# Attention with a gated feed-forward: six homes for evicted query and key tiles, the bound in other banks and another place, and moved sums

## The chip, the cores and the metric

The kernel runs on one core of one Trainium2 chip. The metric is the device time of one execution in microseconds (us); times are medians of several runs. The engines are named as in the profile: PE is TensorE (PEld its weight loads), DVE is VectorE, ACT is ScalarE, POOL is GpSimd, and SP issues most of the transfers.

## The reference

The kernel computes a layernorm of x (2048 tokens, 512 columns), a 32-head softmax attention on it, and beside that a SwiGLU feed-forward of width 1792; the result is x plus the attention's output times the silu of the feed-forward's.

```python
def _A_ref(x, wqkv, wo):                      # 32 heads of 16
    qkv = (x @ wqkv).reshape(B, S, 3, H, Dh) ...
    scores = einsum("bhqd,bhkd->bhqk", q, k) * Dh ** -0.5
    o = einsum("bhqk,bhkd->bhqd", softmax(scores), v)
    return o.transpose(...).reshape(B, S, D) @ wo
def _B_ref(x, w_gate, w_up, w_down):
    return (silu(x @ w_gate) * (x @ w_up)) @ w_down
x = A_x                                        # 1 x 2048 x 512
xn = _layernorm(x)
return x + _A_ref(xn, wqkv, wo) * silu(_B_ref(xn, w_gate, w_up, w_down))
```

## The kernel before

**Order.** The order of the instructions on each engine is that of the program text: the scheduler is in manual mode, so an instruction stands in its engine's queue where the code calls it, and an engine works its queue in order. What an instruction waits for (data, a free buffer, a free PSUM bank) is worked out from the tiles that it names.

**Precision.** Matmuls run in a reduced fp32 format. Each operand is split into a high part, which ScalarE casts, and a low part, which VectorE makes by subtraction; a product is high by high, high by low and low by high. Such pairs are xh and xl, whi and wlo, twh and twl (the first and second `split_turn` outputs), guh and gul (the split gate and up weights).

**Prologue.** The first part, up to about 98 us, works on four blocks of 512 tokens: layernorm and transposes on PE, VectorE and ScalarE, the projections to values (`value_tile`) for all of the blocks, and those to queries and keys (`feature_tile`) for the first two. The tiles have numbers `at` from 0 to 31; `step(at, late, ...)` registers a small piece of work that is run before (late 0) or after (late 1) the tile `at`, in the order in which the steps are registered. Blocks 2 and 3 have the tiles 24 to 31. The high and low halves of the normed block 3 are xt_179 and xt_180, in the profile just xt. The value tiles are copied by ScalarE to the staging tile `vt` and stored to v_d. The last of them is accumulated in the bank `extra`.

**Six jobs.** Then the queries and keys of blocks 2 and 3, and two slices of gate and up, are computed by `strassen(i)` for six jobs, in the order qk, qk, feed-forward, qk, qk, feed-forward (below: the first to the last job). A job makes seven products in place of eight: `product` is six matmuls of 128x512 into one of four PSUM banks out of a ring of six (`ring_of`; two of the six are `extra` and `acc`). The products are combined from `spots`: m1 and m5 by ScalarE's copies (line 1030 and 1037), w, u3, c12 and c21 by VectorE (1031, 1041, 1017, 1011), c22 by GpSimd (1042). `sums(i)` makes four sums and differences of job i's raw weights in raw_x (lines 940 to 943), `whole_of(i)` and `summed_of(i)` split the raw weights and the sums in two parts (957, 958, 950, 951, 964, 965). `split_turn(k)` does the same for four sums of the token blocks, made in wide_mr and facc. `between` is a piece that a job runs between its third and its fourth product: the stores of a normed block (`store_x`), the first loads of the attention, or the bound.

**Evictions.** Each of the four qk jobs ends four tiles of 128 features by 512 tokens, 16 evictions in all. `feature_out` squares the tile (ScalarE, 971), casts its high part (ScalarE, 972) and subtracts the low part (VectorE, 973, GpSimd for one of four) into a tile `parts`, stores both parts to q_d or k_d through SP's queue (975), and keeps the maximum of the squares in `top` (VectorE, 976). There are four buffers of `parts`. The first eviction of a job runs in the job, the three others are put in the list `behind` and run in the next job, after its second product.

**The bound.** The softmax uses one shift for everything, worked out from the largest squares. `bound` sums `top` over features with eight small matmuls (`squares`, line 819) into the banks bankx and banky, takes two maxima (1142) and adds them (1143); `spread_shift` makes the shift and a flag out of it and sends it to where the attention reads it. The banks bankx and banky are also those of gate and up, whose matmuls (`fill`, line 290) take the high and low weights guh and gul of `split_gu` (219 and 220); two operations of VectorE (314, 315) end a slice.

**Branch and main loop.** The flag is loaded on every engine (`values_load`, 1153), and a branch (1155) jumps over a general path that isn't taken here. Behind it the pieces still in `behind` run (`first_half`, `second_half`), and the main loop of scores, exponentials and products with the values begins, with the rest of the feed-forward as filler between its matmuls. Its order comes from a planner and isn't touched.

## Time and profile before

| | |
|---|---|
| median of 3 runs | 1398.55 us (1397.57 to 1399.06) |
| profiled execution | 1397.1 us |
| its span | 1395.3 us |
| mean granted TensorE clock | 0.996 |
| TensorE busy | 1376.7 us |
| ScalarE busy | 1169.9 us |
| VectorE busy | 777.1 us |
| GpSimd busy | 146.1 us |

The profile is of one execution, and starts of rows are in us from the span's start. A timeline row gives start, duration, engine, line, operation, output and inputs with their shapes, how many instructions it gathers, and in brackets how long the engine had stood idle before it and what released it. "PEq" or "DVEq" as a releaser is the engine's own sequencer. A waits row gives who waited for whom, the total, how often, and the longest. A windows row gives the busy time and the number of instructions of each engine in a stretch, then the granted clock as a share of full speed, the busy share of the DMA engines, and what they moved. Line numbers of rows are those of the kernel before.

### The profile page before, as it was taken

To read this page: it belongs to the slowest core of one execution; us is meant where nothing else is said; L and a number is where in the kernel's file an instruction comes from. 1 tells how busy PE (TensorE), PEld (TensorE's weight loads), DVE (VectorE), ACT (ScalarE), POOL (GpSimd) and SP (SyncE) were. 2 spreads that over 40 slices of the span, in tenths; PEclk is the share of its full clock that TensorE was granted. 3 is DMA by queue.
4 is the path that set the end of the run, shared out by engine and by line. 5 is a ranking of instruction groups with operands and counts; after the bars stand their busy time and mean duration, and the time that the engine had idled before them with its cause. 6 is when DMAs were issued, how large, how long until landed. Compare 5 with 4: busy or idle time off the path is not lost.

```text
span 1395.3 us, 27442 instructions
## 1 busy us (share of the span) xinstructions
PE 1376.7 (99%) x11020; PEld 854.3 (61%) x11020; DVE 777.1 (56%) x1228; ACT 1169.9 (84%) x1942; POOL 146.1 (10%) x182
## 2 busy tenths in 40 slices
PE   9998899999999999999999999999999999999998
PEld 7877665555665556656566556565556665566555
DVE  7797765535544554466535544563556446656556
ACT  6756468899988998899888889998899889998875
POOL 4335310000000000000010000000100000000142
PEclk9999999999999999999999999999999999999999
DMA  9888665633236433524534355246424113225652
GB/s 300 279 274 263 208 166 118 125 71 93 66 69 137 107 71 76 131 75 105 132 96 99 94 118 119 55 100 124 113 52 97 41 39 74 59 74 160 204 182 84
DMA packets 142868, 169.13 MB, mean 121 GB/s; under 512 B 13850, under 2 KB 87602, under 8 KB 141967
## 3 DMA queue, kind: packets, MB, share of 16 engines
q1 hardware_dynamic: 135198, 141.99, 41.1%
q0 software_dynamic: 7056, 24.78, 5.3%
q8 instruction: 89, 1.46, 0.5%
q10 hardware_dynamic: 480, 0.54, 0.1%
q14 instruction: 45, 0.36, 0.1%
HBM read 119.78 MB, written 45.37 MB: 118 GB/s over the span
## 4 chain that ended last, share of the span: by engine, by line
PE 87%; DVE 0%; DVEq 0%; issue 0%
PE acc L525 32%; PE bankx L290 29%; PE score L1250 10%; PE single L1250 9%; PE banky L290 6%; PE spare L1250 0%; PE spare L1305 0%; PE banky L1305 0%; PE score L1305 0%; DVE y L1312 0%; PE single L1305 0%; DVE facc L1008 0%; DVE y L1318 0%; DVEq L1365 0%
## 5 line engine op out<-in xcount | busy, mean ns | idle before, releaser
L525 PE MATMUL acc<-pr,vst 128*17 128x512 f32 x4096 | 459.5, 593 | 0.0
L1260 ACT ACTIVATE pr<-single 128x512 f32<-128x512 f32 x722 | 411.0, 607 | 9.4 <-PE single L1250 3.8
L1253 ACT ACTIVATE pr<-score 128x1024 f32<-128x1024 f32 x354 | 365.8, 1033 | 27.5 <-PE score L1250 11.0
L525 PEld LDWEIGHTS acc<-pr,vst 128*17 128x17 f32 x4096 | 109.6, 97 | 283.3 <-issue 282.1
L290 PE MATMUL bankx<-fx,guh 64*128 64x512 f32 x832 | 275.4, 393 | 1.4 <-PEq L1155 1.4
L290 PE MATMUL banky<-fx,guh 64*128 64x512 f32 x832 | 275.6, 393 | 0.0
L1257 DVE COPY pr<-spare 128x512 f32<-128x512 f32 x158 | 109.2, 691 | 227.7 <-PE spare L1250 211.8
L1250 PE MATMUL score<-qst,kst 50*128 50x512 f32 x866 | 225.4, 414 | 1.0 <-DVE facc L1008 1.0
L1250 PE MATMUL single<-qst,kst 50*128 50x512 f32 x921 | 213.7, 399 | 0.0
L1270 ACT ACTIVATE pr<-pr 128x512 f32<-128x512 f32 x357 | 198.2, 644 | 0.0
L290 PE MATMUL banky<-wd,hh 64*128 64x512 f32 x672 | 198.0, 392 | 0.0
L290 PE MATMUL bankx<-wd,hh 64*128 64x512 f32 x672 | 197.7, 391 | 0.0
L1257 DVE COPY pr<-single 128x512 f32<-128x512 f32 x199 | 136.9, 688 | 100.3 <-PE single L1250 98.5
L1250 PEld LDWEIGHTS score<-qst,kst 50*128 50x128 f32 x866 | 101.9, 184 | 127.9 <-ACT pr L1260 70.5
L1260 ACT ACTIVATE pr<-score 128x512 f32<-128x512 f32 x158 | 94.9, 601 | 100.9 <-PE spare L1250 92.6
L290 PEld LDWEIGHTS bankx<-fx,guh 64*128 64x128 f32 x832 | 155.3, 187 | 20.2 <-issue 2.2
L290 PE MATMUL bankx<-fx,gul 64*128 64x512 f32 x416 | 163.7, 394 | 0.0
L290 PE MATMUL banky<-fx,gul 64*128 64x512 f32 x416 | 163.6, 393 | 0.0
L290 PEld LDWEIGHTS banky<-fx,guh 64*128 64x128 f32 x832 | 155.4, 187 | 2.5
L1250 PEld LDWEIGHTS single<-qst,kst 50*128 50x128 f32 x921 | 116.6, 185 | 24.6 <-ACT pr L1260 9.7
L290 PEld LDWEIGHTS bankx<-wd,hh 64*128 64x128 f32 x672 | 125.1, 186 | 10.4
L290 PEld LDWEIGHTS banky<-wd,hh 64*128 64x128 f32 x672 | 125.2, 186 | 0.3
(293 smaller groups left out, 1769.1 us busy)
## 6 DMA issues: line engine op xcount, KB each, us to landing
fx<-xt_d SPq DMA_DIRECT2D x48, 512.0 KB
gur<-in_B_w_gate_dram SPq DMA_DIRECT2D x52, 256.0 KB
gur<-in_B_w_up_dram SPq DMA_DIRECT2D x52, 256.0 KB
kst<-k_d SPq DMA_DIRECT2D x192, 64.0 KB
qst<-q_d SPq DMA_DIRECT2D x192, 64.0 KB
q_d<-parts SPq DMA_DIRECT2D x16, 512.0 KB
k_d<-parts SPq DMA_DIRECT2D x16, 512.0 KB
xt_d<-xt POOLq DMA_DIRECT2D x6, 1024.0 KB, 6.6
```

What stands on the lines that cost most here:

```text
L290: mm(bank, lhs[h], rhs[h], start=start, stop=stop)
L525: mm(acc[h * 32:h * 32 + DH + 1], v[:, kt % CT, h * (DH + 1):(h + 1) * (DH + 1)], probs[2 * i + h // 2][:, h % 2], start=tiles[0] == at == ...
L1250: mm(banked[h], k[r, j, kc * P:(kc + 1) * P], q[r, j], start=True, stop=True)
L1253: exps.append(act(pr, both_banks, AF.Exp, scale=0.25))
L1257: dve.tensor_copy(pr[:, h], banked[h])
L1260: exps.append(act(pr[:, h], banked[h], AF.Exp, scale=0.25))
L1270: exps.append(act(part, part, AF.Exp, scale=0.25))
```

## The change

Six things are changed.

1. `feature_out` has six homes for its tiles in place of four: the four buffers of `parts`, and two regions of `vt`. Counted from 1, the evictions 4, 5, 10, 11 and 16 go to `vt`.
2. `bound` takes its banks as an argument: two of the ring of six that the last job doesn't use at that point, in place of bankx and banky. It runs after the last job's fourth product in place of before it.
3. In the last job the gate products (both pieces of `fill`), with `spread_shift` between them, come directly after `bound`, ahead of the last three products. Of `other_half` only the sum c12 stays in the job; its tanh, the two multiplications and the store come after the branch. `split_gu(1)` comes after c12.
4. The sums of the first job's weights are made by VectorE; those of the second job stay on GpSimd, and wait until VectorE has made the second half of the fourth token sum (`fourth`).
5. The steps of tiles 26 to 31 are placed anew: the token sums and their splits come one or two tiles later, the fourth one after the last value tile.
6. The stores of the normed blocks 2 and 3 (two transfers each, GpSimd's queue) run in the second and third job rather than the first and second.

```diff
-        def squares(m, sq):
-            mm(banks[m // 4][(m % 4) * 32:(m % 4) * 32 + 32], ind, sq, start=True, stop=True,
+        def squares(m, sq, to):
+            mm(to[m // 4][(m % 4) * 32:(m % 4) * 32 + 32], ind, sq, start=True, stop=True,
                skip_group_check=True)
...
+        def fourth():
+            turns_x["made"] = dve.tensor_add(wide_mr, wide_mr, b21[1]).ins.name
...
         def sums(i):
...
-            pool.tensor_add(s[:, 0], raw[:, 0], raw[:, 1])
-            pool.tensor_sub(s[:, 1], s[:, 0], raw[:, 2])
-            pool.tensor_sub(s[:, 2], raw[:, 2], raw[:, 0])
-            pool.tensor_sub(s[:, 3], raw[:, 3], s[:, 1])
+            engine = pool if i else dve
+            made = engine.tensor_add(s[:, 0], raw[:, 0], raw[:, 1])
+            if i == 1:
+                tc.add_manual_dep(made.ins, turns_x["made"], settled, reason="GpSimd would hold VectorE up")
+            engine.tensor_sub(s[:, 1], s[:, 0], raw[:, 2])
+            engine.tensor_sub(s[:, 2], raw[:, 2], raw[:, 0])
+            engine.tensor_sub(s[:, 3], raw[:, 3], s[:, 1])
...
         def feature_out(m, b, src, pooled):
-            parts = p3.tile([P, 2, TB], F32R, tag="parts", name="parts")
+            evicted.append(m)
+            at = len(evicted) % 6
+            if at < 4:
+                parts = p3.tile([P, 2, TB], F32R, tag="parts", name="parts")
+            else:
+                n = (at - 4) * 2 * TB
+                parts = vt.rearrange("p g t c -> p (g t c)")[:, n:n + 2 * TB].rearrange("p (s t) -> p s t", s=2).bitcast(F32R)
...
             def other_half():
-                dve.tensor_add(c12, bank[2], w)
+                if more:
+                    dve.tensor_add(c12, bank[2], w)
...
             product(bank[3], summed[2], t3, True, False)
+            if not more:
+                bound([ring_of[(4 * i + n) % 6] for n in (4, 5)])
...
             else:
-                product(bank[2], summed[3], b22, False, True)
-                other_half()
                 fill(3 * DC // 2)
                 spread_shift(ring_of[(4 * i + 4) % 6])
+                fill(3 * DC // 2)
+                product(bank[2], summed[3], b22, False, True)
+                dve.tensor_add(c12, bank[2], w)
                 split_gu(1)
-                fill(3 * DC // 2)
                 product(bank[0], whole[2], b21, False, True)
                 product(bank[3], whole[0], t4, False, True)
                 behind.append(first_half)
                 behind.append(second_half)
+                behind.append(other_half)
...
-        step(26, 1, dve.tensor_sub, wide_mr, upper_x, lower_x)
+        step(27, 1, dve.tensor_sub, wide_mr, upper_x, lower_x)
         for j in range(2):
-            step(27, j, dve.tensor_sub, lower_x, lower_x, b11[j])
+            step(28, 0, dve.tensor_sub, lower_x, lower_x, b11[j])
         step(28, 0, dve.tensor_sub, upper_x, upper_x, lower_x)
-        step(28, 0, whole_of, 0)
+        step(28, 1, sums, 0)
+        step(28, 1, whole_of, 0)
         step(28, 1, split_turn, 0, upper_x)
         step(29, 0, split_turn, 1, lower_x)
-        step(29, 0, summed_of, 0)
-        step(29, 1, split_turn, 2, wide_mr)
-        step(30, 0, dve.tensor_sub, wide_mr, b21[0], upper_x)
-        step(30, 0, dve.tensor_add, wide_mr, wide_mr, b21[1])
-        step(30, 1, split_turn, 3, wide_mr)
-        step(27, 0, sums, 0)
+        step(29, 1, summed_of, 0)
+        step(30, 0, split_turn, 2, wide_mr)
+        step(31, 1, dve.tensor_sub, wide_mr, b21[0], upper_x)
+        step(31, 1, fourth)
+        step(31, 1, split_turn, 3, wide_mr)
...
-        def bound():
+        def bound(to):
             for m in range(8):
-                squares(m, top[m])
+                squares(m, top[m], to)
             for j in range(2):
-                dve.reduce_max(peak[:, j:j + 1], banks[j], axis=AX.X)
+                dve.reduce_max(peak[:, j:j + 1], to[j], axis=AX.X)
...
-            strassen(i, {0: partial(store_x, 2), 1: partial(store_x, 3), 3: first_loads, len(jobs) - 1: bound}.get(i))
+            strassen(i, {1: partial(store_x, 2), 2: partial(store_x, 3), 3: first_loads}.get(i))
```

On VectorE, around the value tiles of block 3, before; xt_180 is the block's low half, the line 742 is that of all the steps, and facc and wide_mr hold the token sums:

```order
L742 TENSOR_TENSOR xt_180<-facc,xt_179 128x512 x3
L742 TENSOR_TENSOR wide_mr<-facc 128x1024
L742 TENSOR_TENSOR facc<-facc,xt_177 128x1024
L742 TENSOR_TENSOR xt_180<-facc,xt_179 128x512
L742 TENSOR_TENSOR facc<-facc,xt_178 128x1024
L742 TENSOR_TENSOR facc<-facc 128x1024
```

and now:

```order
L742 TENSOR_TENSOR xt_180<-facc,xt_179 128x512 x4
L742 TENSOR_TENSOR wide_mr<-facc 128x1024
L742 TENSOR_TENSOR facc<-facc,xt_177 128x1024
L742 TENSOR_TENSOR facc<-facc,xt_178 128x1024
L742 TENSOR_TENSOR facc<-facc 128x1024
L944 TENSOR_TENSOR raw_x<-raw 128x256
L947 TENSOR_TENSOR raw_x<-raw_x,raw 128x256
L948 TENSOR_TENSOR raw_x<-raw 128x256
L949 TENSOR_TENSOR raw_x<-raw,raw_x 128x256
```

The fourth subtraction for xt_180 has moved ahead of two of the token sums, and the four sums of the first job's raw weights have come in behind the token sums.

On ScalarE, at the end of the value tiles, before; twh are the high parts of the token sums, extra is the bank of the last value tile, and the copy to spots is the first of the first job:

```order
L895 COPY vt<-ps 128x8x4x16
L934 CAST twh_992<-wide_mr 128x1024
L895 COPY vt<-ps 128x8x4x16
L934 CAST twh_1012<-wide_mr 128x1024
L895 COPY vt<-extra 128x8x4x16
L1030 COPY spots<-ps 128x512
```

and now:

```order
L970 CAST part<-raw_x 128x1024
L937 CAST twh_992<-wide_mr 128x1024
L895 COPY vt<-ps 128x8x4x16
L895 COPY vt<-extra 128x8x4x16
L937 CAST twh_1029<-wide_mr 128x1024
L1042 COPY spots<-ps 128x512
```

The copy out of extra has moved ahead of the cast of the fourth token sum.

On TensorE, in the last job at the end of the bound's small matmuls, before; acc and ps are ring banks:

```order
L819 LDWEIGHTS ind
L819 MATMUL banky<-top_171,ind 32x512
L1002 MATMUL acc<-twh_992,part 128x512
L1002 MATMUL acc<-twl_993,part 128x512
L1002 MATMUL acc<-twh_992,part 128x512 x2
L1002 MATMUL acc<-twl_993,part 128x512
L1002 MATMUL acc<-twh_992,part 128x512
L1002 MATMUL ps<-xt_179,part 128x512
```

and now:

```order
L819 LDWEIGHTS ind
L819 MATMUL ps<-top_171,ind 32x512
L290 MATMUL bankx<-fx,guh 128x512
L290 MATMUL banky<-fx,guh 128x512
L290 MATMUL bankx<-fx,guh 128x512
L290 MATMUL banky<-fx,guh 128x512
L290 MATMUL bankx<-fx,gul 128x512
L290 MATMUL banky<-fx,gul 128x512
```

What follows the last small matmul was the job's fourth product and is now the gate products with guh and gul; the small matmuls write a ring bank.

On VectorE, in the last job from the shift to the branch, before; s_226, flag and shift are the shift's steps, ga the gate's, guh and gul the split weights of the next gate slice, facc and raw_x those of the job:

```order
L1021 SCALAR_TENSOR_TENSOR raw_x<-raw_x,facc 128x512
L1129 TENSOR_REDUCE s_226<-ps 1x1
L1130 TENSOR_SCALAR s_226<-s_226 1x1
L1131 TENSOR_SCALAR flag<-s_226 1x1
L1132 TENSOR_SCALAR shift<-row,s_226 1x512
L219 CAST guh<-gur 128x1024
L220 TENSOR_TENSOR gul<-gur,guh 128x1024
L314 SCALAR_TENSOR_TENSOR ga<-th,bankx 128x512
L315 SCALAR_TENSOR_TENSOR ga<-ga,banky 128x512
L1153 TENSOR_LOAD flag
L1155 COMPARE_AND_BRANCH
```

and now:

```order
L1055 TENSOR_TENSOR spots<-acc,spots 128x512
L1144 TENSOR_REDUCE s_226<-ps 1x1
L1145 TENSOR_SCALAR s_226<-s_226 1x1
L1146 TENSOR_SCALAR flag<-s_226 1x1
L1147 TENSOR_SCALAR shift<-row,s_226 1x512
L314 SCALAR_TENSOR_TENSOR ga<-th,bankx 128x512
L315 SCALAR_TENSOR_TENSOR ga<-ga,banky 128x512
L1082 TENSOR_TENSOR facc<-ps,spots 128x512
L219 CAST guh<-gur 128x1024
L220 TENSOR_TENSOR gul<-gur,guh 128x1024
L1168 TENSOR_LOAD flag
L1170 COMPARE_AND_BRANCH
```

The sum of c12 (line 1082 in the changed kernel) and the split of the next slice have moved behind the two gate operations, directly ahead of the branch; the two multiplications into raw_x have gone from here.

## Rows read from the trace of the kernel before

**Rows 1.** Page, busy time of each engine: us, share of the span, instructions.
```profile
PE 1376.7 (99%) x11020; PEld 854.3 (61%) x11020; DVE 777.1 (56%) x1228; ACT 1169.9 (84%) x1942; POOL 146.1 (10%) x182
```

**Rows 2.** TensorE's waits: what for, us in total, times, longest.
```profile
PE banky L819 <- DVE top L976: 3.1, 2, 2.4
PE extra L1002 <- ACT spots L1030: 2.3, 1, 2.3
PE extra L1002 <- ACT vt L895: 1.9, 1, 1.9
PE ps L814 <- DVE xt L742: 1.7, 3, 0.8
PE ps L1002 <- DVE parts L973: 1.6, 1, 1.6
PE bankx L290 <- PEq L1155: 1.4, 1, 1.4
...
PE score L1250 <- DVE facc L1008: 1.0, 1, 1.0
```

**Rows 3.** Windows: us, busy of PE, PEld, DVE, ACT, POOL; clock, DMA share, GB/s.
```profile
164.00:168.00 4.00, 3.24 (x8) 1.93 (x7) 3.96 (x6) 0.94 (x2) 0.00 (x0) 0.50 1.01 380
168.00:172.00 4.00, 4.00 (x18) 2.93 (x18) 2.15 (x5) 0.38 (x1) 1.28 (x1) 0.69 0.23 90
184.00:188.00 4.00, 4.00 (x24) 3.71 (x21) 3.38 (x5) 2.97 (x5) 3.84 (x4) 0.57 0.67 203
```

**Rows 4.** Timeline of VectorE to the second job: start, us, operation, [idle before <-releaser].
```profile
78.78 1.82 DVE L742 TENSOR_TENSOR xt<-raw_x,xt 128x512 fp32r<-128x512 f32 x2
...
90.46 1.23 DVE L742 TENSOR_TENSOR facc<-facc,xt 128x1024 f32<-128x1024 f32 x1
...
92.75 1.75 DVE L742 TENSOR_TENSOR facc<-facc,xt 128x1024 f32<-128x1024 f32 x1
...
109.47 0.69 DVE L1041 TENSOR_TENSOR spots<-ps,spots 128x512 f32<-128x512 f32 x1 [0.88 <-PE ps L1002]
...
119.06 1.08 DVE L958 TENSOR_TENSOR whole<-raw,whole 128x256 fp32r<-128x256 f32 x3
```

**Rows 5.** Timeline of TensorE, first to last job.
```profile
106.41 0.50 PE L1002 MATMUL extra<-twh,part 128*128 128x512 f32 x1 [1.88 <-ACT vt L895]
...
112.05 0.39 PE L1002 MATMUL ps<-twh,whole 128*128 128x512 f32 x1
...
154.71 1.54 PE L1002 MATMUL extra<-xt,odd 128*128 128x512 f32 x6
...
160.77 0.40 PE L819 MATMUL bankx<-top,ind 128*32 128x512 bf16 x4
...
176.65 0.39 PE L290 MATMUL bankx<-fx,gul 64*128 64x512 f32 x1
```

**Rows 6.** Timeline of GpSimd, the sums of the third job's weights.
```profile
114.00 0.73 POOL L942 TENSOR_TENSOR raw_x<-raw 128x256 f32<-128x256 f32 x1
```

**Rows 7.** Timeline of ScalarE, casts of evictions 13, 14 and 16.
```profile
157.83 0.58 ACT L972 CAST parts<-ps 128x512 fp32r<-128x512 f32 x1 [5.04 <-DMA q_d<-parts]
...
160.24 0.62 ACT L972 CAST parts<-facc 128x512 fp32r<-128x512 f32 x1 [1.29 <-DMA q_d<-parts]
...
163.35 0.62 ACT L972 CAST parts<-facc 128x512 fp32r<-128x512 f32 x1 [0.20 <-DMA q_d<-parts]
```

**Rows 8.** Timeline of VectorE, fifth job to the branch.
```profile
165.54 0.68 DVE L219 CAST guh<-gur 128x1024 fp32r<-128x1024 f32 x1
166.26 1.23 DVE L220 TENSOR_TENSOR gul<-gur,guh 128x1024 fp32r<-128x1024 f32 x1
...
178.50 0.69 DVE L315 SCALAR_TENSOR_TENSOR ga<-ga,banky 128x512 f32<-128x512 f32 x1
182.21 0.69 DVE L1008 SCALAR_TENSOR_TENSOR facc<-facc,extra 128x512 f32<-128x512 f32 x1 [3.03 <-DVEq L1155]
```

**Rows 9.** Page, DMA issues: count, KB each, us from issue to landing.
```profile
xt_d<-xt POOLq DMA_DIRECT2D x6, 1024.0 KB, 6.6
```

More of the change, by code (lines that the diff above doesn't have):

```diff
@@ L976, in feature_out @@
             dve.tensor_max(top[m], top[m], sq)
-        behind = []
-        ring_of = []
+        behind, ring_of, evicted = [], [], []
         def strassen(i, between=None):
```

## The prediction

> **What bounds the kernel now.** I read the page's busy line first: TensorE is busy 1376.7 us of 1395.3, VectorE 777.1 [rows 1]. So only time in which TensorE stands still, or runs at the lower of its clock's two levels, can be won. The main loop, from about 183 us to the end, is a gapless stream in which the change moves nothing, so all of the difference has to come from the first 190 us. Second, TensorE's waits by releaser [rows 2]: in this part there are 13.0 us of them on seven lines that the change touches. In order of time they are: the value tiles of blocks 2 and 3 behind VectorE's layernorm (1.7), the first job's fourth product behind an eviction (1.9), the third job behind ScalarE (2.3), the fifth job's ring bank behind a cast (1.6), the bound's small products behind the last maxima (3.1), and the two around the branch (1.4 and 1.0). Third, the windows [rows 3]: from 164 to 172 us the granted clock averages 0.50 and then 0.69. [...] Another such stretch, 0.57, follows the branch.
>
> The profiled execution took 1397.1 us, 1.8 more than its span, and the median of the three runs is 1398.55. I sum against the profiled one and take the difference off the median, since everything changed lies inside the span.
>
> **First job: moved steps and sums.** The waits at the value tiles go if all works. The longest of the three, 0.8, is for the last subtraction that makes xt_180, which now follows its three fellows directly (two subtractions of 1.2 us less ahead of it on VectorE, as the one at 90.46 [rows 4]). The other two, 0.9 together, are for the pair at 78.78, which took 1.82 us beside GpSimd's first sums [rows 4]; those sums leave GpSimd. And 1.9 us go at extra, since ScalarE's copy out of extra no longer stands behind the cast of twh_1012, which waits for VectorE. That is 3.6. What is late next is VectorE. Its chain in the first job ends with the sum u3 at 109.47 [rows 4], which waited 0.88 us for TensorE; without that it starts at 108.59 and ends at 109.28. The seventh product, which writes the bank that u3 reads, began at 112.05 [rows 5]; so it can come at most 2.8 earlier. Does the chain itself grow? The four sums that VectorE takes over are a quarter-size each: three such operations take 1.08 us, so four take 1.4 [rows 4]. Against that, three subtractions of 1024 columns ran at 1.65 to 1.75 us beside GpSimd's sums, where a free one took 1.23 [rows 4]; those sums now wait behind fourth, so 3 x 0.5 = 1.5 comes back. That is even. But the same GpSimd sums now run later, beside the split of twl_1030, odd and u3, and lengthen one or two of them by the same 0.5. I take 0.4 off: **2.4 us won**, bounds 1.5 (two operations lengthened, and the next job's split weights late by 0.3) and 3.6 (VectorE not in the way).
>
> The row says that such a neighbour stretches an operation by 0.5 us [rows 4]. [...]
>
> **Six homes.** A cast of eviction n waits until the transfer of n-4 has left its buffer; now it waits for n-6. Evictions 7 and 8 then wait for 1 and 2, long landed, and the 2.3 us at extra in the third job [rows 2] goes: **2.3 won**, since ScalarE's queue there holds nothing else that is late. In the fifth job eviction 13's cast waited 5.04 us for eviction 9's transfer [rows 7]; it now looks at 7's, and TensorE's 1.6 us behind it [rows 2, 5] goes: **1.6 won**. The bound from below is nothing, if another transfer is as late. The two homes in the value staging tile are covered by its stores, which are over before.
>
> **Bound in banks of its own, three products later.** The last of eight small products waits for the last maximum. Eviction 16's cast, at 163.35, can't come before eviction 10's transfer lands; that landing is what released the cast at 160.24 [rows 7]. From the start of the last cast to the end of VectorE's cast to guh there were 2.87 us (163.35 to 166.22), to the end of gul 4.14 [rows 7, 8]. So in the new order, and on the old time axis, guh is there at 163.11 and gul at 164.38. TensorE has the four products from 154.71 on done at 160.23, at 1.38 each [rows 5]. Its stretch from there to gul is 4.15; in it lie eight small products, about 1.0 us by four in 0.40 with their loads [rows 5], and two pairs of gate products, 0.46. So 2.7 us of waiting are left against 3.1 [rows 2]: **0.4 won**. If the transfers land in time, all but nothing is waited: 3.1 won. The gate products that now fill the place behind the small products need guh and gul, which stand on VectorE behind the maximum; that is why the wait is not hidden.
>
> **The clock.** At 164 to 168 us TensorE was busy 3.24 us at 0.50, which cost 1.62; at 168 to 172 it was 4.00 at 0.69, which cost 1.24 [rows 3]. Together 2.9 won if no dip stands there. But 2.7 us of wait remain in nearly the same place, and after the branch a wait of that size was followed by 0.57 over 4 us, a cost of 1.7 [rows 3]. I take such a dip as likely: **1.2 won**, bounds 0 and 2.9.
>
> **The tail before the branch.** The products of c12, which came before the gate stretch, stand behind it, and VectorE's sum c12 and the split of gul (with guh) come after the two gate results. Let T be the end of the last gate product, 177.04 before [rows 5]. TensorE then has three products, 4.2, then the branch, 1.35, and filler 0.7: it is at the score at T+6.3. VectorE ends the second gate operation at T+2.14 (178.50+0.69), then c12 0.6, guh 0.7, gul 1.2: T+4.7. Behind the branch it stood still 3.03 us, then first_half's operation of 0.69 [rows 8]. The score waits for that, as it did for 1.0 us [rows 2]: it can start at about T+8.6. That is 2.3 of waiting where there was 1.0: **1.3 lost**. Bounds: 0 lost, and 2.0 if other_half's tanh, now also behind the branch, gets ahead of something. other_half's store and the memsets on GpSimd behind it are needed some 20 us later and cost nothing.
>
> [...] The row says a branch costs VectorE 3.03 us of standing still [rows 8]. [...]
>
> **Small.** Five waits fewer each save the slower first product behind a wait, 0.50 against 0.39 [rows 5]: **0.5 won**. The two stores of x blocks move one job later, to where the evictions' transfers run; I put that at nothing, and its price is rival E.
>
> **Sum.** 2.4 + 2.3 + 1.6 + 0.4 + 1.2 - 1.3 + 0.5 = 7.1 us, so 1397.1 becomes 1390.0 and the median 1398.55 becomes **1391.4**.
>
> **The rivals.** **B**, transfers land early: fewer collisions ahead of eviction 10, no wait at the bound and no dip. Then 2.7 and 1.7 come on top: a gain of 11.5, 1387.0; for it speaks that evictions start earlier, against it that four jobs' casts waited for transfers. **C**, the clock stays low as long as before, and GpSimd's moved sums cost the first job their full bound: 1.2 and 0.9 less, a gain of 5.0, 1393.5; 1394.3 if the stretch behind the branch is longer too. For it speaks that the wait at the bound keeps nearly its size. **D**, the homes were not the limit: the transfers are, each cast waits as long one home later, and the clock falls as before. Without 2.3, 1.6, 0.4 and 1.2 the gain is 1.6: 1396.9, no measurable change. For it speaks the DMA share of 1.01 at 164 to 168 [rows 3], against it that the wait of 5.04 is for a transfer four evictions back. **E**, slower: the x-block stores, 1 MB each and 6.6 us from issue to landing [rows 9], get ahead of eviction 10's transfer. TensorE pays in full for each us that this lands later, since the bound waits for eviction 16 and that for 10. Slower by more than 0.2% from 9.9 us later; two stores in its way are 13.2: 1404.6. Against it: the stores are issued 30 us before. **F**, VectorE's branch is cheap: the tail's wait is gone, 2.3 more, 1389.1.
>
> **How the numbers follow.** A change under 0.2%, about 2.8 us, can't be told from none. Forecast 50%, B 15%, C 22%, D 7%, E 3%, F 3%. Only D lies within 0.2%, only E above: faster 0.90, same 0.07, slower 0.03. The range runs from 1386.8, B's time with a little of the first term's upper bound, to 1394.6, C's upper end with as much; it leaves out D, E and the outer part of B.
>
> **What would show it.** Right: no waits at the value tiles, at extra in the first job and in the third; eviction 13's cast not waiting for a transfer; a wait of 2 to 3 us at the small products or at the first gate products behind guh; a clock below 1 for about 4 us behind it; the score waiting 2 us or more for VectorE. Wrong: a wait of the second job for its split weights behind GpSimd's sums (first term), eviction 16's cast released by something other than a transfer (fourth term, B), a clock of 1 up to the branch (fifth), casts in the second to fourth job waiting for transfers (D, E).

## The result, and the profile after

The changed kernel takes 1400.74 us in the median of 20 runs (1399.16 to 1402.51), the kernel before, in 20 runs beside it, 1397.63. The ratio is 1.0022, with a 95% interval from 1.0015 to 1.0029: slower by 3 us, where 1391.4 was forecast. The profiled execution took 1399.16 us, its span 1397.4. Line numbers below are those of each kernel's own code; in the changed one 1013 stands for 1002, 988 for 976, 1055 for 1041, 1265 for 1250, 1268 for the exponential (1253).

The page's busy line, which answers to [rows 1]:

```profile
PE 1377.4 (99%) x11020; PEld 852.8 (61%) x11020; DVE 779.1 (56%) x1232; ACT 1169.7 (84%) x1942; POOL 141.7 (10%) x178
```

TensorE is as busy as before within 1 us, so the difference is again mostly in its waits. Those of the changed kernel, in the form of [rows 2]:

```profile
PE ps L819 <- DVE top L988: 4.3, 2, 2.2
PE score L1265 <- ACT pr L1268: 3.4, 1, 3.4
PE score L1265 <- DVE facc L1019: 1.5, 1, 1.5
PE ps L1013 <- DVE spots L1055: 1.5, 3, 0.8
PE bankx L290 <- PEq L1170: 1.3, 1, 1.3
...
PE bankx L290 <- DVE guh L219: 0.6, 1, 0.6
PE ps L1013 <- ACT spots L1042: 0.5, 1, 0.5
```

All that was to go has gone: the value tiles' 1.7 us (0.3 is left, behind ScalarE), the 1.9 and the 2.3 at extra, the 1.6 at a ring bank. In their place the jobs have five short waits behind spots, for u3 and for ScalarE's copies, 2.4 us together (1.5, 0.5 and 0.4). The small products wait 4.3 us rather than 3.1, and one line is new and large: the second scores behind the branch wait 3.4 us for ScalarE. What ScalarE waited for there is in its timeline (start, duration, operation, idle time before and releaser):

```profile
159.08 0.62 ACT L984 CAST parts<-facc 128x512 fp32r<-128x512 f32 x1 [4.25 <-DMA q_d<-parts]
...
161.54 0.62 ACT L984 CAST vt<-facc 128x512 fp32r<-128x512 f32 x1 [1.31 <-DMA q_d<-vt]
...
185.86 1.02 ACT L1268 ACTIVATE pr<-score 128x1024 f32<-128x1024 f32 x1 [8.41 <-DMA h_d<-raw_x]
```

The third row is the main loop's first exponential. ScalarE had been idle for 8.4 us, and what released it is the store of h_d out of raw_x. SP's timeline shows when that store was issued:

```profile
183.73 0.33 SPq L1034 DMA_DIRECT2D h_d<-raw_x  x1
```

It is other_half's store, which the change put behind the branch. It lands about 2 us after its issue, and the exponential starts then. TensorE's seventh product of the first job, against 112.05 in [rows 5]:

```profile
109.61 0.50 PE L1013 MATMUL ps<-twh,whole 128*128 128x512 f32 x1 [0.24 <-DVE spots L1055]
```

TensorE's two stretches at the lower clock, 0.50 where it is 1.00 just ahead of them and behind them, in the form of [rows 3], before:

```profile
163.60:170.40 6.80, 5.90 (x13) 3.90 (x13) 5.51 (x10) 1.34 (x3) 0.74 (x1) 0.50 0.80 296
184.10:187.50 3.40, 3.40 (x20) 3.13 (x18) 3.21 (x4) 2.41 (x4) 3.24 (x4) 0.50 0.60 190
```

and now:

```profile
162.80:169.60 6.80, 5.62 (x23) 3.52 (x24) 4.86 (x9) 0.33 (x1) 1.27 (x1) 0.50 1.08 368
186.70:190.10 3.40, 3.16 (x15) 3.01 (x17) 2.71 (x4) 3.08 (x6) 3.24 (x4) 0.50 1.07 225
```

By starts in the two traces the changed kernel is ahead by 2.4 us at that seventh product, by 4.0 at the last job's third product (155.18 against 159.19), and by 1.9 at the first score (181.18 against 183.10). At 200 us it is behind by 1.6, and so it stays for most of the loop (2.1 at the end). So where the forecast had 6.3 us (2.4 + 2.3 + 1.6), 4.0 were there. Half of these were lost between the third product and the first score, and 3.5 us more went between 181 and 192 us.

### The profile page after: what moved, and what is told of

Its sections match the earlier page's. It is cut to its first block, busy times and chain, and to the rows that moved or that the text cites. A ratio compares the mean times of both kernels' runs of the same rounds, so it can differ in the third digit from the quotient of the medians.

```text
span 1397.4 us, 27445 instructions
## 1 busy us (share of the span) xinstructions
PE 1377.4 (99%) x11020; PEld 852.8 (61%) x11020; DVE 779.1 (56%) x1232; ACT 1169.7 (84%) x1942; POOL 141.7 (10%) x178
## 4 chain that ended last, share of the span: by engine, by line
PE 86%; DVE 0%; DMA 0%; ACT 0%; DVEq 0%; issue 0%; ACTq 0%
PE acc L525 32%; PE bankx L290 28%; PE score L1265 10%; PE single L1265 8%; PE banky L290 6%; PE spare L1265 1%; PE spare L1320 0%; PE banky L1320 0%; DMA h_d<-raw_x 0%; ACT pr L1268 0%; PE score L1320 0%; DVE raw_x L1033 0%; DVE y L1327 0%; PE single L1320 0%; DVE facc L1024 0%; DVE facc L1019 0%
```

## The experiments

Each run has its own runs of the kernel before beside it (medians 1396.8 to 1397.4), so ratios are compared where a few us matter. One per cent is 14 us.

**One address.** The last job's g2 in a tile of the gate's pool, not in raw_x:

```diff
-            g2 = wide_mr[:, 0] if more else raw_x[:, 0]
+            g2 = wide_mr[:, 0] if more else two.tile([P, TB], F32, tag="ga", name="g2")
```

> The changed kernel (1400.7), with one address changed: the last job's product g2, which other_half stores behind the branch, lies in a tile of the pool of gate results rather than in raw_x. Nothing moves on any engine. Theory (the loss sits behind the branch: the main loop's first exponential takes over memory of the prologue's pool, and so waits for the store out of raw_x): ScalarE's wait for the store goes, TensorE's 3.4 us at the second pair of scores too, and 1 to 1.7 us of low clock behind it; 1395.5 to 1397. Rival (the loss is the bound's longer wait and the order of the last job): another wait takes the store's place, 1400 to 1401.

Measured 1399.27 us, ratio 1.0014 (1.0003 to 1.0024), and its eleven runs are spread from 1395.9 to 1402.1. TensorE's waits, and VectorE's timeline behind the branch:

```profile
PE ps L819 <- DVE top L988: 4.5, 2, 2.6
PE single L1265 <- DVE pr L1272: 3.5, 1, 3.5
PE score L1265 <- DVE facc L1019: 2.7, 1, 2.7
```

```profile
184.37 1.23 DVE L220 TENSOR_TENSOR gul<-gur,guh 128x1024 fp32r<-128x1024 f32 x1
189.58 0.43 DVE L234 CAST wd<-wdr 128x512 fp32r<-128x512 f32 x1 [3.98 <-DMA kst<-k_d]
```

The wait for the store is gone, as the theory said, and the first exponential waits for nothing but its scores. But the time is not: VectorE now stands for 4.0 us at the cast of the first down weights (wd), and TensorE for 3.5 us behind a copy of VectorE's that is queued behind this cast. The releaser is named as a load of kst, which shares a semaphore with the load of wdr; the cast waits for wdr. SP issued that load only behind the two stores of the last job, which wait for VectorE. Its place in the queue isn't all of it: it was issued at 183.3 and landed about 6 us later, where the one of the changed kernel, issued at 184.1, took about 3. Behind TensorE's wait the clock is at 0.50 from 192 to 199 us, which it is not in the changed kernel. The rival is not borne out by this, but neither is the theory's size.

**The last job as before**, the rest as changed:

```diff
...
-            if not more:
-                bound([ring_of[(4 * i + n) % 6] for n in (4, 5)])
...
+                product(bank[2], summed[3], b22, False, True)
+                other_half()
                 fill(3 * DC // 2)
                 spread_shift(ring_of[(4 * i + 4) % 6])
-                fill(3 * DC // 2)
-                product(bank[2], summed[3], b22, False, True)
-                dve.tensor_add(c12, bank[2], w)
                 split_gu(1)
+                fill(3 * DC // 2)
...
-                behind.append(other_half)
...
-            strassen(i, {1: partial(store_x, 2), 2: partial(store_x, 3), 3: first_loads}.get(i))
+            strassen(i, {1: partial(store_x, 2), 2: partial(store_x, 3), 3: first_loads, len(jobs) - 1: partial(bound, banks)}.get(i))
```

> The changed kernel with the last job as it was before: the bound in bankx and banky ahead of the fourth product, the gate products behind the third product of bank 2, all of other_half ahead of the branch. Homes, steps, sums and stores stay changed. Theory: the store is ahead of the branch again, so the 3.4 us go; the last maximum comes 1.8 us earlier than in the kernel before, since the last cast does; about 1395.8, as far as e1. Rival (late transfers are what costs, wherever the store stands): 1399 to 1401.

Measured 1394.71 us, ratio 0.9984 (0.9975 to 0.9993): 5.3 us below the changed kernel by the ratios. So the last job's new order, with all that it moved behind the branch, costs more than the whole loss. The wait at the small products is longer than in either kernel:

```profile
PE banky L819 <- DVE top L988: 5.6, 2, 3.7
```

**Four homes:**

```diff
-            at = len(evicted) % 6
+            at = 0
```

> The changed kernel with four homes for evictions, as before. Theory (the homes won what was forecast): the waits of 2.3 us in the third job and 1.6 us in the fifth come back, less up to 0.9 us of VectorE's waits that they hide, and the last cast waits for eviction 12 at about 163.4: 1402.5 to 1404.5. Rival (transfers, not homes, are the limit): 1400 to 1401.5.

Measured 1401.5 us, ratio 1.0029 (1.0018 to 1.0041). The waits of the third and the last job are back at 2.9 and 1.8 us, but those at the small products and gate products shrink to 3.0 from 4.9 and the one for the exponential to 2.1. In the changed kernel the homes win about 1 us in all, which is not clear of none: what they win is waited for again at the bound. The time is the upper edge of the rival's range, and at the bound the transfers are indeed the limit.

**The stores of blocks 2 and 3 where they were:**

```diff
-            strassen(i, {1: partial(store_x, 2), 2: partial(store_x, 3), 3: first_loads}.get(i))
+            strassen(i, {0: partial(store_x, 2), 1: partial(store_x, 3), 3: first_loads}.get(i))
```

> The changed kernel with the stores of the normed blocks 2 and 3 in the first and second job, as before. Theory (they made evictions 9 and 10 land 1.3 us late): the casts of 15 and 16 start 1.3 us earlier, TensorE's wait at the small products is 3.6 rather than 4.9 us: about 1399.4. Rival (the early stores collide with the first evictions' transfers and the weights' loads): no earlier landing, a wait in the second or third job, 1400.7 to 1403.

Measured 1396.43 us, ratio 0.9996 (0.9987 to 1.0005): 3.6 us by the ratios, more than the theory's 1.3. ScalarE's cast of eviction 16, and TensorE's waits:

```profile
157.46 0.62 ACT L984 CAST vt<-facc 128x512 fp32r<-128x512 f32 x1 [1.09 <-DMA q_d<-vt]
```

```profile
PE score L1265 <- DVE facc L1019: 2.7, 1, 2.7
PE score L1265 <- ACT pr L1268: 2.5, 1, 2.5
...
PE ps L819 <- DVE top L988: 0.9, 1, 0.9
PE bankx L290 <- DVE guh L219: 0.8, 1, 0.8
```

The cast starts at 157.46 rather than 161.54, so the transfer of eviction 10 lands 4.1 us earlier, and the waits of 4.9 us at the bound become 1.9 (with 0.2 for gul). Moving 4 MB of stores one job later is what made it late. SP's timeline shows how. The changed kernel:

```profile
139.12 6.19 SPq L185 DMA_DIRECT2D kst<-k_d  x6
...
154.24 0.93 SPq L987 DMA_DIRECT2D q_d<-vt  x2
```

and this run:

```profile
138.32 2.75 SPq L185 DMA_DIRECT2D kst<-k_d  x6
...
150.41 1.42 SPq L987 DMA_DIRECT2D q_d<-vt  x2
```

The first of the two q_d stores is eviction 10's. It takes about as long in both runs (7.3 us from its issue to the cast, and 7.1), but is issued 3.8 us later in the changed kernel. The moved stores are not in its way: the last of them, issued at 128.3, had landed 12.5 us later, 13 us before eviction 10 was issued. What they slow are the stores to k_d that are issued beside them: the last two of the job land 12.7 and 14.0 us after their issue rather than 7.9 and 8.2. SP's first six loads of K (line 185) take 6.2 us rather than 2.8, since they stand 2.0 us for that landing and 1.5 for other transfers; and eviction 10 stands behind these loads on SP's queue. Neither this run nor the kernel before has a wait at line 185 from 126 to 158 us; the changed kernel's largest is:

```profile
SPq L185 <- DMA k_d<-parts: 2.0, 2, 1.7
```

All the other kernels with the late stores (e1, e2, e3 and e13) have it too, at 1.5 to 2.2 us, and none of those with the early ones.

**Both undone**, the edits of e2 and e4; then that kernel with the edit of e3, and with the sums as before:

```diff
-            engine = pool if i else dve
+            engine = pool
...
-            if i == 1:
-                tc.add_manual_dep(made.ins, turns_x["made"], settled, reason="GpSimd would hold VectorE up")
...
-        step(28, 1, sums, 0)
...
+        step(27, 0, sums, 0)
```

> The changed kernel with both parts undone that the first runs point to: the last job as before, and the stores of blocks 2 and 3 in the first and second job. Homes, sums and steps stay changed. Theory (two separate losses, the store behind the branch with what the last job's new order brings, 6 us, and the late landings, 4 us): the small products wait 1.5 to 2 us rather than 5.6, the clock dips less; 1390 to 1392. Rival (one loss, seen twice: what the landing wins is lost again at the bound in its old place): 1394 to 1396.

> e5 with four homes. Theory (with the stores out of the way the homes are worth the two waits of 2.3 and 1.6 us, and the cast of eviction 16 waits for 12): 3 to 5 us slower than e5, 1394 to 1396. Rival (the homes only move the wait to the bound, as in e3): within 1 us of e5.

> e5 with the sums of the first job's weights back on GpSimd, two tiles earlier, and those of the second job not held back. Steps stay in their new order. Theory (the first term's two halves, of which the sums carry the subtractions at 78 and 92 us): the two waits of 0.9 us at block 2's value tiles come back, and VectorE's three long subtractions: 1 to 2 us slower than e5. Rival (VectorE's u3 is late in three later jobs anyway and hides it): within 0.5 us of e5.

Measured 1391.35 (e5, ratio 0.9960, 0.9946 to 0.9974), 1397.05 (e6, 1.0000, 0.9991 to 1.0009) and 1389.86 us (e7, 0.9951, 0.9937 to 0.9965). The losses add up: e5 is the changed kernel less 8.7 us, against 5.3 and 3.6 of the two edits alone. With the transfers out of the way the homes are worth 5.7 us. In e6 the wait of the third job is back, and the one at the small products is longer (2.5 in e5):

```profile
PE extra L1013 <- ACT spots L1041: 3.3, 1, 3.3
PE banky L819 <- DVE top L988: 3.2, 2, 2.3
```

The waits are not all of the 5.7. Behind the first of them TensorE runs at the lower clock, which it does neither in e5 nor in the kernel before in that job:

```profile
129.60:136.40 6.80, 5.43 (x13) 4.27 (x14) 5.01 (x8) 5.15 (x7) 2.67 (x2) 0.50 1.06 352
```

TensorE is busy for 5.4 us there at half the clock, so 2.7 us are lost.

The sums on VectorE win nothing; e7 is 1.5 us faster without them by the medians, which neither of its expectations had. It has 1.4 us of waits at block 2's value tiles again, but the seventh product of the first job starts at 109.35 in e7 and at 109.32 in e5, so what won the first term were the moved steps. And in e5 ScalarE's cast of the second job's sums waited 2.1 us for GpSimd's held sums, in e7 for nothing:

```profile
109.29 1.05 ACT L970 CAST part<-raw_x 128x1024 fp32r<-128x1024 f32 x1 [2.10 <-POOL raw_x L949]
```

```profile
107.35 1.06 ACT L968 CAST part<-raw_x 128x1024 fp32r<-128x1024 f32 x1
```

**The sums not held**, as e5 but without the wait on `fourth`:

```diff
-            if i == 1:
+            if i == 9:
                 tc.add_manual_dep(made.ins, turns_x["made"], settled, reason="GpSimd would hold VectorE up")
```

> e5 without the hold on the second job's sums (they start on GpSimd as soon as their weights are there); the first job's stay on VectorE. Theory (the hold is what cost e5 its 1.5 us against e7: the second job's split of sums and with it ScalarE's copies came late): 1389.5 to 1390.5, as e7. Rival (the four sums on VectorE cost it): 1391 to 1392, as e5.

Measured 1392.4 us, ratio 0.9964: no better than e5. It was not the hold; with the first job's sums on VectorE, the waits come back at other places (0.9 us for a split of sums, 1.3 for a copy of ScalarE's). That VectorE's own 1.5 us are the cost agrees with all three runs; more is not shown.

**All ahead of the branch.** The stores early, g2 in a gate tile as in e1, evictions 15 and 16 behind the last job's own copies and sums, the first load of down weights in the job, and the job in this order:

```diff
-            while behind:
+            while len(behind) > (0 if more else 2):
                 behind.pop(0)()
...
+            while not more and behind:
+                behind.pop(0)()
...
             else:
-                fill(3 * DC // 2)
-                spread_shift(ring_of[(4 * i + 4) % 6])
-                fill(3 * DC // 2)
                 product(bank[2], summed[3], b22, False, True)
                 dve.tensor_add(c12, bank[2], w)
                 split_gu(1)
+                fill(3 * DC // 2)
+                bound([ring_of[(4 * i + n) % 6] for n in (4, 5)])
+                fill(3 * DC // 4)
+                spread_shift(ring_of[(4 * i + 4) % 6])
+                fill(3 * DC // 4)
+                load_wd(0, 0)
                 product(bank[0], whole[2], b21, False, True)
+                first_half()
                 product(bank[3], whole[0], t4, False, True)
-                behind.append(first_half)
-                behind.append(second_half)
-                behind.append(other_half)
+                second_half()
+                other_half()
```

> The changed kernel with the early stores and another order of the last job: the evictions 15 and 16 stand on ScalarE and VectorE behind the job's copies and sums, the third product of bank 2 and one half of the gate products ahead of the bound, the other half, two products and all of first_half, second_half and other_half behind it and ahead of the branch; g2 in a gate tile; the first load of down weights issued ahead of the branch. Theory (all waits from the fourth product to the second score are for casts, for splits behind maxima, and for pieces behind the branch): TensorE waits for nothing from 152 us to the branch, the first score comes at about 171 us rather than 181, no low clock: 1384 to 1388. Rival (the landing of eviction 10 or the branch's own 3 us on VectorE take the place): 1390 or more.

Measured 1394.78 us, ratio 0.9982 (0.9973 to 0.9991). TensorE waits for nothing at the bound, but there is a new wait, and SP's timeline shows it:

```profile
PE score L1267 <- SPq L1173: 6.2, 1, 6.2
PE ps L1146 <- DVE sm L1161: 2.0, 1, 2.0
```

```profile
175.79 0.32 SPq L1034 DMA_DIRECT2D h_d<-g  x1
180.38 0.72 SPq L212 DMA_DIRECT2D gur<-in_B_w_gate_dram  x1
```

SP issues the last store at 175.79, and its next transfer behind the branch comes 4.6 us later. Until then the first score can't start: it waits on what SP announces behind the branch. Of the 4.6 us, 1.3 lie ahead of SP's own branch (177.1), and 2.7 between it and SP's first instruction behind it (179.8). The store's landing is not what is waited for: from 178.3 to 180 us no DMA packet moves at all, and in the kernel before SP stood 2.6 us at the branch (178.8 to 181.3) without a store just ahead of it. The loss is that SP comes to the branch late, 4.2 us after TensorE's last product, since it first issues the stores, and the last of them waits for VectorE's last multiplication (to 175.8). VectorE, with the same work ahead of its branch, is late with it: it starts again at 179.8.

**other_half in the job**, in the changed order with early stores (e4 with its store ahead of the branch):

```diff
-                dve.tensor_add(c12, bank[2], w)
+                other_half()
                 split_gu(1)
...
-                behind.append(other_half)
```

> The changed kernel with the early stores (e4, 1396.4) and all of other_half in the job, ahead of the split and of the branch; the rest of the last job in its new order. Theory (the store behind the branch is the larger part of what the new order costs): ScalarE doesn't wait for the store, TensorE's 2.5 us at the second scores go and the low clock behind them, two operations more on VectorE ahead of the branch cost up to 1.4: 1392.5 to 1394.5. Rival (as in e8 the store's landing then holds SP's branch and the first score): 1395.5 to 1397.

Measured 1396.19 us, ratio 0.9992 (0.9983 to 1.0001), its runs from 1393.5 to 1398.4: no gain over e4, as the rival said, though by another engine:

```profile
PE score L1263 <- DVE facc L1019: 5.1, 1, 5.1
```

```profile
173.05 1.23 DVE L220 TENSOR_TENSOR gul<-gur,guh 128x1024 fp32r<-128x1024 f32 x1
177.99 0.69 DVE L1019 SCALAR_TENSOR_TENSOR facc<-facc,extra 128x512 f32<-128x512 f32 x1 [3.71 <-DVEq L1168]
```

The store's wait is gone, and VectorE, with two operations more, ends its work 2.4 us later than TensorE; then it stands 3.7 us at the branch, and the first score waits 5.1 us for it.

**Stores behind, but out of the way.** e8 with the two stores and the products ahead of them behind the branch again, c21 ahead of it, the split of gul behind the shift, and the load of down weights ahead of the bound; then the same with e7's sums:

```diff
-                split_gu(1)
                 fill(3 * DC // 2)
+                load_wd(0, 0)
                 bound([ring_of[(4 * i + n) % 6] for n in (4, 5)])
                 fill(3 * DC // 4)
                 spread_shift(ring_of[(4 * i + 4) % 6])
+                split_gu(1)
                 fill(3 * DC // 4)
-                load_wd(0, 0)
                 product(bank[0], whole[2], b21, False, True)
                 first_half()
                 product(bank[3], whole[0], t4, False, True)
-                second_half()
-                other_half()
+                dve.tensor_add(c21, bank[3], w)
+                behind.append(second_half)
+                behind.append(other_half)
```

> e8 with what its trace points to: there the first score waited 6.2 us for SP, whose branch stood behind the two stores of the last job and their landing, and TensorE 2.0 us for a maximum behind the split of gul. Here both stores and the products ahead of them stand behind the branch again, but out of memory that the main loop doesn't take over (a gate tile), c21 ahead of the branch, the split behind the shift. Theory (what the branch waits for is what SP has under way): the first score at 171 to 173 us, no wait for SP over 2 us: 1385 to 1388. Rival (it is the branch itself that costs SP and ScalarE 4 us and more): 1391 to 1395.

> e9 with the sums on GpSimd as in e7. Theory (the gain of e7 lies in the second job and adds up): 1 to 2 us faster than e9. Rival (it is lost at the casts' landings): within 0.5 us of e9.

Measured 1389.15 (e9, ratio 0.9942, 0.9929 to 0.9956) and 1386.67 us (e10, 0.9925, 0.9912 to 0.9939). Both are faster than either kernel, the second by 10.6 us than the one before. The sums make 2.5 us here. What is left in e10 at the branch:

```profile
PE bankx L290 <- PEq L1173: 3.1, 1, 3.1
PE score L1267 <- DVEq L1173: 1.0, 1, 1.0
```

The branch itself, 3.1 us on TensorE (3.5 in e9), is now the largest of its waits. e9's time lies between its theory's range and the rival's. The first score comes at 174.3 us rather than at 171 to 173, and SP still stands 3.5 us at the branch (168.2 to 171.7), with no store just ahead of it. In e8 most of SP's 2.7 us went by with no packet moving, so the landing of what SP has under way isn't the main part of this cost. Whether it makes the 0.8 us more of e9 is open.

**The changed kernel less what was found behind the branch**, e1 with the first load of down weights ahead of the last two products; and with early stores too:

```diff
+                load_wd(0, 0)
                 product(bank[0], whole[2], b21, False, True)
...
-    load_wd(0, 0)
```

> e1 (1399.3, its runs 6 us apart) with the first load of down weights issued ahead of the last two products rather than behind the branch and the two stores on SP's queue. Theory (what took the store's place in e1 is VectorE's 4.0 us for those weights, whose load lands early in some runs and late in others): the wait goes, and the runs lie within 2 us of each other; 1394.5 to 1396.5. Rival (the low clock behind the bound and the branch holds the time, whatever waits there): 1398 to 1400.

> e13 with the early stores of blocks 2 and 3: the changed kernel with its order, its sums and its steps, less the three things found behind the branch and on the queues. Theory (the losses are separate): e4's 1396.4 less TensorE's 2.5 us for the store and some low clock, 1391 to 1393.5. Rival (the first score's 2.7 us for VectorE grow into it): 1394 to 1396.

Measured 1395.04 (ratio 0.9987, 0.9978 to 0.9996) and 1391.36 us (0.9961, 0.9947 to 0.9975). VectorE in e13 goes from gul to wd without a wait:

```profile
183.98 1.22 DVE L220 TENSOR_TENSOR gul<-gur,guh 128x1024 fp32r<-128x1024 f32 x1
185.12 0.42 DVE L234 CAST wd<-wdr 128x512 fp32r<-128x512 f32 x1
```

That closes e1: the store and the load of weights behind it make 4.9 us by the ratios. (The runs of e13 still lie 3.4 us apart, not 2.) The early stores make 3.6 more. e14 keeps the changed order, sums and homes, and its waits and windows show the bound nearly covered and the clock at full there; a stretch at 0.50 is left behind the branch, where TensorE had waited 2.8 us:

```profile
PE score L1265 <- DVE facc L1019: 2.8, 1, 2.8
...
PE bankx L290 <- DVE guh L219: 0.8, 1, 0.8
PE ps L819 <- DVE top L988: 0.6, 1, 0.6
PE bankx L290 <- DVE gul L220: 0.5, 1, 0.5
```

```profile
160.00:164.00 4.00, 3.12 (x24) 2.13 (x24) 3.49 (x6) 0.00 (x0) 0.28 (x1) 1.00 1.08 383
164.00:168.00 4.00, 4.00 (x30) 2.83 (x29) 0.96 (x4) 0.57 (x1) 1.40 (x2) 1.00 0.94 294
176.00:180.00 4.00, 4.00 (x21) 4.00 (x21) 3.75 (x6) 2.07 (x4) 3.84 (x4) 0.50 0.35 132
```

## Why the prediction was wrong, point by point

**Two steps failed, and both had been put at nothing.** The first: "other_half's store and the memsets on GpSimd behind it are needed some 20 us later and cost nothing." I had asked who reads the stored values, and not who takes over the memory. The tiles of the exponentials come from a pool that is given the memory of the prologue's pool, and its first use waits for all users of that pool, raw_x among them: 8.4 us of idle ScalarE and 3.4 of TensorE. On SP's queue the load of the first down weights stood behind the same store, and its wait showed as soon as the first was gone (e1). Together 4.9 us (changed kernel against e13). The second: the moved x-block stores, "I put that at nothing". The rival E named the end of the chain, a later landing of eviction 10 that TensorE pays, but had the stores in the way of that transfer itself, asked for 9.9 us and got 3%. By the traces they slowed the stores to k_d instead, SP's loads of K stood for these, and eviction 10 was issued 3.8 us late behind them (e4). As a term it was 4.1 us of landing and 3.4 to 3.6 us of time (three pairs: e4, e5 against e2, e14 against e13). No row of SP's queue and no DMA share of the third job, where the stores went, was read for it; the share there, 1.1 at 128 to 132 us, was in the trace of the kernel before. That SP's queue is the path is read from the traces; no run moves the loads of K alone.

**First term, 2.4 won.** Right at its place: the seventh product starts 2.4 us earlier, and VectorE is late next (0.24 us). But the lower bound's reason came true as well: the second job's split waited for GpSimd, and 1.1 of it were given back in the second job. The half of it that I ascribed to the sums was wrong: they lose 1.5 to 2.5 us (e7, e10). VectorE's and GpSimd's timelines in the changed kernel:

```profile
100.90 1.22 DVE L938 TENSOR_TENSOR twl<-wide_mr,twh 128x1024 fp32r<-128x1024 f32 x1
...
105.80 1.68 DVE L938 TENSOR_TENSOR twl<-wide_mr,twh 128x1024 fp32r<-128x1024 f32 x1 [1.17 <-ACT twh L937]
```

```profile
105.69 0.72 POOL L947 TENSOR_TENSOR raw_x<-raw_x,raw 128x256 f32<-128x256 f32 x1
106.37 1.72 POOL L948 TENSOR_TENSOR raw_x<-raw 128x256 f32<-128x256 f32 x1
```

A split of 1024 columns beside the sums took 1.68 us where a free one took 1.22, as the row for the forecast had it, and the seventh product came 2.4 us earlier. The split began 0.11 us into a sum of 0.72 and took 0.46 longer than the free one; the next sum, begun 0.57 us after the split, took 1.0 longer than the one ahead of it. Ahead of the seventh product it is the only operation of VectorE that the sums lengthened.

**Homes, 2.3 and 1.6 won.** Both waits are gone. In each of the two jobs TensorE then waits 0.4 us for u3 instead, so by starts 2.8 of the 3.9 are left at the last job's third product. Where the transfers land in time the homes are worth 5.7 us (e5 against e6), of which the lower clock in e6 makes 2.7; in the changed kernel they are worth about 1 us (e3), since the bound waits for what they bring forward.

**The bound, 0.4 won.** It lost 1.8: 4.9 us of waits against 3.1. The mechanism, the last cast behind the landing of eviction 10, was right; the landing moved. In e4 it is 1.9, in e14 1.9 too, below the 2.7 forecast.

**The clock, 1.2 won.** The dip at the bound was not halved: both stretches at 0.50 are there as before. TensorE was busy 5.62 and 3.16 us in them, against 5.90 and 3.40 before, and half of the difference, 0.3, was won.

**The tail, 1.3 lost.** VectorE stood 2.4 us at the branch rather than 3.0, and the first score waited 1.5 us rather than 2.3, so 0.5 was lost in waiting. Rival F is out: the wait didn't go. The branch instruction itself takes 0.07 us on VectorE, but VectorE stands 2.4 to 4.4 us around it in the kernels above.

**Small, 0.5 won.** There are no fewer waits to save a slow first product behind: twelve from 60 to 215 us, where the kernel before had ten.

**The sum.** In the traces, 4.0 at the last job's third product, less 1.8 at the bound, plus 0.3 of the clock, less 0.5 and 3.4 behind the branch, is 1.4 lost; at 200 us the changed kernel is behind by 1.6. e14, which has every part of the change without the two failures, and besides the load of down weights ahead of the branch, takes 1391.36 us; 1391.4 was forecast. That is partly luck. By its ratio e14 gains 5.4 us (3.5 to 7.4) where the forecast gain was 7.1, since the kernel before took 1396.8 beside it and 1398.55 beside the prediction; and the weight sums moved to VectorE, counted as part of the gain, are a loss.

## What to carry to other kernels

Of a store that is moved, ask three things: who reads it, who is given the memory that it reads from, and what stands behind it on its queue. Ahead of a branch, what stands behind it is the branch of the engine that issues it (e8, where SP came to its branch 4.2 us after TensorE's last product). A bulk transfer that moves into a stretch where the DMA engines are full (a share of 1.1 here) is a term of the sum. Its price can be paid far from it: here the loads that stood for a slowed store held up a queue, and a transfer behind them that was issued 13 us after the bulk had landed. When a change bundles parts, undo each on a base where nothing else hides it: the same homes were worth about 1 us in one kernel and 5.7 in another, and half of the 5.7 was the clock.

## What was unexpected of the hardware

The idle time that TensorE spends at the same branch differs from kernel to kernel with the code around it: 0.2 us in e14, 0.8 in e8, 1.3 to 1.4 in the two kernels, 3.1 in e10 and 3.5 in e9. VectorE's goes from 2.4 to 4.4 (e9). SP's, from its branch to its next instruction, goes from 2.6 to 3.6 in all sixteen kernels, with a store just ahead of it or without. What sets it is not settled by these runs. The load of the first down weights, 256 KB, landed about 3 us after its issue in the profiled execution of the kernel before and about 6 in that of e1, where fifteen of the sixteen signals of its landing had come within 3.1 us and the last was 3 us behind them; the kernels whose main loop waits for it have runs up to 6 us apart.
